# Float32r matmuls read their moving columns from the two halves of a tile in turn

## The chip, the cores and the metric

One core of a Trainium2 chip runs the whole program. The metric is device time in microseconds (us) from launch to the last result, the median of the runs made; lower is better.

## The reference

The inputs are q, k and v of 8 batches, 8 heads, 576 positions and 64 dimensions, and the weights of two feed-forward blocks. A retention layer (attention without softmax, with a decay per head) feeds a maxout block, and that a bilinear block:

```python
def reference(**kwargs):
    # retention: scores = q k^T / sqrt(D), times gamma^(i-j) for j <= i, times v
    x = np.ascontiguousarray(attn_out.transpose(0, 2, 1, 3)).reshape(B * S, H * D)  # 4608 x 512
    # maxout: d_ff = 768
    h = np.maximum(np.maximum(x @ w1, x @ w2), x @ w3)
    x = h @ w_out
    # bilinear: d_ff = 1024
    a = x @ w1
    b = x @ w2
    h = a * b @ w3
    return (h @ w_out).astype(np.float32)
```

## The kernel before

The kernel works in stages, and in all of them TensorE (PE) does the products, ScalarE (ACT) and VectorE (DVE) read the results out of the PSUM banks, and GpSimd (POOL) takes some of the elementwise work.

**How one product is made.** The retention itself (lines 343 to 404) uses plain float32 matmuls. Everything behind it uses the type float32r: each operand is split into a high part (a copy rounded to float32r, `copy_r`, line 92) and a low part (the remainder, `low`, line 95), and a product of two operands is three matmuls, high by high, low by high, high by low, that all add into one PSUM bank. A matmul has a stationary operand (128 columns, loaded first) and a moving operand that streams past it, 512 or 256 columns wide. In memory the moving columns stand next to each other, four bytes each.

**The stages.** (1) For each of 9 blocks of 512 tokens, `products` (line 478) multiplies the token block, the moving operand, with the three maxout weights; 12 matmuls of 512 columns fill a bank, and `maximum` (line 488) reads it: a copy by ACT for the first weight, a maximum by DVE for the other two. In between PE makes the retention products of the next block. An order written out by hand (`ORDER`) sets the first two blocks, and due times the rest. (2) The product with `w_out` of the maxout block, as a fast matrix product with seven multiplications in place of eight (`Z_ORDER`, line 526), in five groups of tokens, four with 512 columns and one with 256. `snap_z` and `keep_z` (lines 765 and 770) read the banks. (3) The product of the two last weights, `ps_w` (line 912), 192 matmuls of 512 columns. (4) The two bilinear factors, again with seven products (line 1176), in ten visits, eight with 512 columns and two with 256; `snap`, `plus` and one multiplication (lines 1154, 1159 and 1209) read the banks. (5) The last product (`add_o`, line 1223), in 18 steps of 84 matmuls of 256 columns; `snap_o`, `plus_o` and a copy (lines 1231, 1236 and 1283) read the banks.

All matmuls of stages 2 to 5 are issued by one helper, `product` (line 709, the matmul on line 715), those of stage 1 on line 486. PE works its matmuls off in the order written. The first stage has six banks for the products, the later ones eight, so that the reading of one bank lies beside the filling of others.

Of the kernel before, what the change touches and what calls it, by code (L numbers as in the profile page):

```python
# [13 lines left out]
AF = mybir.ActivationFunctionType  # L14
ALU = mybir.AluOpType
# [72 lines left out]
def tile_retention_maxout_bilinear(ctx: ExitStack, tc, a, out):  # L88
    nc = tc.nc
    chunks = chunk_list()  # L90

    def copy_r(dst, src):
        nc.scalar.activation(dst, src, AF.Copy)  # L93
# [3 lines left out]

    def load(dst, src):
        nc.sync.dma_start(out=dst, in_=src)  # L99

    first_ps = ctx.enter_context(ExitStack())
    ps_mm = first_ps.enter_context(tc.tile_pool(name="ps_mm", bufs=6, space=PSUM))
# [17 lines left out]
    def bank(name):  # L120
        return ps_mm.tile([P, 512], F32, tag="mm", name=name)
# [75 lines left out]
    w1h = [w1_p.tile([P, 3, 4, P], F32R, name=f"w1h{f}") for f in range(KF1)]  # L197
    w1l = [w1_p.tile([P, 3, 4, P], F32R, name=f"w1l{f}") for f in range(KF1)]
# [279 lines left out]
    def products(t, f, i, cols):  # L478
        xh, xl = xs[t]
        ps = hbs[t, f, i, cols.start] = bank("ps_h")  # L480
        mms = []
        for c in range(4):
            mms += [(w1h[f][:, i, c], xh[:, c, cols]), (w1l[f][:, i, c], xh[:, c, cols])]
        mms += [(w1h[f][:, i, c], xl[:, c, cols]) for c in range(4)]
        for n, (l, r) in enumerate(mms):
            nc.tensor.matmul(ps[:, cols], l, r, start=n == 0, stop=n == len(mms) - 1)  # L486

    def maximum(t, f, i, cols):
        ps = hbs.pop((t, f, i, cols.start))
        if (t, f) not in hbs:  # L490
            hbs[t, f] = hb_p.tile([P, N1], F32, tag="hb", name="hb")
        hb = hbs[t, f][:, cols]
        if i == 0:
            copy_r(hb, ps[:, cols])
        else:
            nc.vector.tensor_tensor(hb, ps[:, cols], hb, ALU.max)  # L496

    def keep(t, f):
        load(h_d[t][:, f], hbs.pop((t, f)))
# [129 lines left out]
    with tc.manual_schedule():  # L629
# [79 lines left out]
        def product(ps, terms, start=True, stop=True, again=False):  # L709

            mms = []
            for lh, ll, rh, rl in terms:
                mms += [(lh, rh), (ll, rh), (lh, rl)]
            for j, (l, r) in enumerate(mms):
                nc.tensor.matmul(ps, l, r, start=start and j == 0, stop=stop and j == len(mms) - 1, skip_group_check=again)  # L715
# [48 lines left out]

        def snap_z(ps, size):
            t = zo_p.tile([P, N1], F32, tag="zs", name="zs", bufs=6)[:, :size]
            nc.scalar.activation(t, ps[:, :size], AF.Copy)
            return t

        def keep_z(j, m, n, ps, other=None):  # L770
            size = z_groups[j][3]
            o = zo_p.tile([P, N1], F32, tag="zo", name="zo", bufs=4)[:, :size]
            if other is None:
                nc.scalar.activation(o, ps[:, :size], AF.Copy)
            else:
                nc.vector.tensor_tensor(o, ps[:, :size], other, ALU.add)
            load(z_d[j][:, m, n * size:n * size + size], o)

        behind_z = {0: [(h_t4, 0)], 1: [(load_h, 1, "b12")], 2: [(load_h, 1, "b21")], 3: [(h_t3, 1), (load_h, 2, "b22")],
# [1 line left out]
        for j, (_, _, _, size) in enumerate(z_groups):  # L781
            Z = {}
            saved = {}
            for n, (x, y) in enumerate(Z_ORDER):
# [4 lines left out]
                ps = Z[bank_of]  # L789
# [115 lines left out]
        ps_w = []  # L905
        for n in range(2 * KF2):
            k, e = divmod(n, 2)
            th, tl = w3t.pop(n)
            for m in range(4 * e, 4 * e + 4):
                if k == 0:  # L910
                    ps_w.append(bank8(f"ps_w{m}"))
                product(ps_w[m], [(th[:, m % 4], tl[:, m % 4], *wo2[k])], k == 0, k == KF2 - 1)
                if k == KF2 - 1:
                    t = w4_p.tile([P, DM], F32, tag="w4", name="w4")
                    copy_r(t, ps_w[m])
                    load(w4_d[:, m], t)
            prepare_34(*[(get_w3t, n + 4)] * (n + 4 < 2 * KF2), *[(get_wo2, k + 2)] * (e == 0 and k + 2 < KF2), lag=2)
            lows()
            if steps:
                steps.pop(0)()  # L920
# [202 lines left out]
        for n, (k, q) in enumerate(visits):  # L1123
            B, size = ops[k % 2], z_groups[k][3]
            if n == 5:
                steps = steps + fetches(visits[7][0])
            elif n == 9:
                steps = steps + late[1]
            elif n != 4:
                steps = steps + rest.pop()  # L1130
                if n == 3:
                    second_q = second_sums()
                    steps += second_q.pop(0)
                elif n == 8:
                    late = last_operands()
                    steps += late[0]
                else:
                    steps += fetches(visits[n + 2][0]) + 3 * [waiting]

            left_ticks = [14]  # L1140

            def tick():
                if n == 4 and left_ticks[0] == 7:
                    steps.extend(second_q[0])
                left_ticks[0] -= 1
                lows()
                for _ in range(1 if n in (4, 5) else 3 if n == 3 or n in (0, 1, 2, 6, 7) and left_ticks[0] % 2 or n == 9 and left_ticks[0] % 2 else 2):
                    if steps:
                        step = steps.pop(0)
                        step()  # L1150
                        if step is waiting:
                            break

            def snap(ps):
                t = work("snap", 5)[:, :size]
                nc.scalar.activation(t, ps[:, :size], AF.Copy)  # L1156
                return t

            def plus(ps, t):
                r = work("c", 6)[:, :size]  # L1160
                nc.vector.tensor_tensor(r, ps[:, :size], t, ALU.add)  # L1161
                return r

            def keep_g(t, half, cols):
                off = half * z_groups[k][2]
                load(g_d[z_groups[k][half]][:, cols, off:off + size], t)

            def times(x, y):
                nc.gpsimd.tensor_tensor(x, x, y, ALU.mult)  # L1169
                return x  # L1170

            for o in (2 * q, 2 * q + 1):
                fs = slice(o % 2 * P, (o % 2 + 1) * P)
                X, V, Y = ([bank8(f"ps_{x}{i}") for i in range(2)] for x in "xvy")

                def add(ps, x, y, start):
                    for i in range(2):
                        (ah, al), (bh, bl) = wsum[i][q][x], B[y]
                        product(ps[i][:, :size], [(ah[:, c, fs], al[:, c, fs], bh[:, c, columns(size)], bl[:, c, columns(size)]) for c in range(2)],
                                start, True, not start)  # L1180

                add(X, "a11", "b11", True)
                p1 = [snap(X[i]) for i in range(2)]
                tick()
                add(V, "a12", "b21", True)
                c11 = [plus(V[i], p1[i]) for i in range(2)]
                tick()
                add(X, "s2", "t2", False)
                g11 = times(*c11)
                u2 = [snap(X[i]) for i in range(2)]  # L1190
                tick()
                add(Y, "s1", "t1", True)
                p5 = [snap(Y[i]) for i in range(2)]
                tick()
                add(X, "s3", "t3", False)
                keep_g(g11, 0, o)
                c22 = [plus(X[i], p5[i]) for i in range(2)]
                g22 = times(*c22)
                tick()
                add(Y, "s4", "b22", False)  # L1200
                c12 = [plus(Y[i], u2[i]) for i in range(2)]
                keep_g(g22, 1, 4 + o)
                g12 = times(*c12)
                tick()
                add(X, "a22", "t4", False)
                c21 = snap(X[0])
                keep_g(g12, 1, o)
                g21 = work("c", 6)[:, :size]
                nc.vector.tensor_tensor(g21, X[1][:, :size], c21, ALU.mult)
                keep_g(g21, 0, 4 + o)  # L1210
                tick()
        for step in steps:
# [17 lines left out]

        def snap_o(ps):
            t = work("snap", 5)[:, :256]
            nc.scalar.activation(t, ps[:, :256], AF.Copy)
            return t

        def plus_o(dst, ps, t):
            nc.vector.tensor_tensor(dst, ps[:, :256], t, ALU.add)

        def open_s(s):

# [13 lines left out]
        for s in range(n_s):  # L1254
            X, V, Y = banks.pop(s)
            ob = obs.pop(s)
# [23 lines left out]
                plus_o(ob[0][:, 256:], Y, u2)  # L1280
                load(out[2 * turn[s] * P:(2 * turn[s] + 1) * P, :], ob[0])
            add_o(X, "a22", "t4", False, s)
            nc.scalar.activation(ob[1][:, :256], X[:, :256], AF.Copy)
            cols = slice(0, DM if s + 1 < n_s else 256)
            load(out[(2 * turn[s] + 1) * P:(2 * turn[s] + 2) * P, cols], ob[1][:, cols])
            gq.pop(s)
# [28 lines left out]
```

## Time and profile before

| | us |
|---|---|
| median of 3 runs | 1266.95 |
| lowest and highest of them | 1266.43, 1274.92 |
| span of the profiled execution | 1265.7 |
| PE busy in it | 1256.2 |
| DVE busy | 885.5 |
| ACT busy | 488.1 |
| POOL busy | 314.1 |

The profile is of one execution, traced from the first to the last instruction; that distance is its span. A matmul's duration in the trace, from its start to its modelled end, is longer than the distance between the starts of two matmuls, since they overlap; the pace is read from the starts, or from a stretch that holds many of them. Idle time of an engine is listed with what ended it.

### The profile page before, as it was taken

The page shows a single profiled execution, that of the slowest core. Times are in us where ns is not written, and L with a number is a line of the kernel's source. Part 1 is how long each engine was busy: PE and PEld are TensorE (multiplying, and loading weights), DVE is VectorE, ACT ScalarE, POOL GpSimd, SP SyncE. Part 2 cuts the span into 40 slices and gives each one's busy share as a digit, 9 for nine tenths or more (in the row PEclk, how much of TensorE's full clock was granted, in tenths as well). Part 3 has the DMA queues.
Part 4 walks back from the last instruction along what each step waited for, and adds up shares of the span by engine and source line. Part 5 has one row for each costly group of instructions (what it writes and reads, how often), then busy time and mean ns, then how long its engine had stood idle before and what let it go on. Part 6 is the DMA issues. An engine that isn't in the chain of part 4 may idle for free.

```text
span 1265.7 us, 22992 instructions
## 1 busy us (share of the span) xinstructions
PE 1256.2 (99%) x8900; PEld 1079.0 (85%) x8900; DVE 885.5 (70%) x1256; ACT 488.1 (39%) x873; POOL 314.1 (25%) x262
## 2 busy tenths in 40 slices
PE   8999999999999999999999999999999999999999
PEld 6888888888888878888888888888998888999998
DVE  5885667666666666366988547776666766899896
ACT  4551122222222212134565454443344343555554
POOL 2111211212111210000000315544243542344443
PEclk9999999999999999999999999999999999999999
DMA  9945788777978795434743733332333314455552
GB/s 210 244 119 118 148 210 211 178 207 182 246 180 175 166 198 154 166 109 151 225 174 122 236 110 125 116 124 103 110 113 133 117 51 160 131 176 159 167 175 101
DMA packets 323793, 199.34 MB, mean 157 GB/s; under 512 B 241634, under 2 KB 279266, under 8 KB 323684
## 3 DMA queue, kind: packets, MB, share of 16 engines
q1 hardware_dynamic: 323684, 197.87, 56.2%
q8 instruction: 70, 1.15, 0.4%
q14 instruction: 39, 0.32, 0.1%
HBM read 131.76 MB, written 66.06 MB: 156 GB/s over the span
## 4 chain that ended last, share of the span: by engine, by line
PE 91%; DMA 3%; DVE 2%; SPq 2%; issue 1%; ACT 1%; POOL 0%; DVEq 0%; POOLq 0%; ACTq 0%
PE ps_h L486 32%; PE ps_x L715 23%; PE ps_y L715 11%; PE ps_v L715 6%; PE ps_X L715 5%; PE ps_Y L715 3%; PE o L384 2%; PE sc L369 2%; PE ps_w L715 2%; SPq L99 2%; PE ps_V L715 1%; DMA raw<-in_moe_w_dram 1%; PE st L404 1%; PE o L391 1%; DMA w<-wo_d 1%
## 5 line engine op out<-in xcount | busy, mean ns | idle before, releaser
L486 PE MATMUL ps_h<-xh,w1h 128*128 128x512 f32 (+1 forms) x664 | 257.3, 389 | 0.0
L486 PE MATMUL ps_h<-xh,w1l 128*128 128x512 f32 (+1 forms) x664 | 254.4, 385 | 0.6 <-DVE w1l L96 0.6
L486 PE MATMUL ps_h<-xl,w1h 128*128 128x512 f32 (+1 forms) x664 | 174.1, 384 | 0.0
L486 PEld LDWEIGHTS ps_h<-xh,w1h 128*128 128x128 f32 x664 | 124.6, 188 | 27.6 <-issue 2.1
L486 PEld LDWEIGHTS ps_h<-xh,w1l 128*128 128x128 f32 x664 | 124.7, 188 | 25.0 <-DVE w1l L96 0.9
L486 PEld LDWEIGHTS ps_h<-xl,w1h 128*128 128x128 f32 x664 | 123.0, 188 | 24.8
L496 DVE TENSOR_TENSOR hb<-ps_h,hb 128x512 f32<-128x512 f32 (+1 forms) x110 | 74.4, 677 | 93.0 <-PE ps_h L486 85.9
L1169 POOL TENSOR_TENSOR c<-c 128x512 f32<-128x512 f32 (+1 forms) x60 | 84.2, 1405 | 174.4 <-DVE c L1161 132.2
L1156 ACT ACTIVATE snap<-ps_x 128x512 f32<-128x512 f32 (+1 forms) x100 | 55.7, 557 | 174.4 <-PE ps_x L715 174.3
L355 POOL TENSOR_TENSOR q<-q,tables 128x512 f32<-128x512 f32 (+1 forms) x31 | 31.4, 1011 | 282.1 <-DMA q<-in_q_dram 164.3
L166 ACT ACTIVATE e<-raw 128x512 f32<-128x512 f32 x64 | 42.9, 670 | 131.8 <-DMA raw<-in_moe_w_dram 90.7
L93 ACT ACTIVATE hb<-ps_h 128x512 f32<-128x512 f32 (+1 forms) x56 | 32.5, 581 | 134.9 <-PE ps_h L486 134.8
L93 ACT ACTIVATE xh<-o 128x512 fp32r<-128x512 f32 (+1 forms) x40 | 22.2, 555 | 110.1 <-PE o L391 68.5
L358 POOL TENSOR_TENSOR v<-v,tables 128x512 f32<-128x512 f32 x40 | 44.6, 1116 | 63.8 <-DMA v<-in_v_dram 59.2
L1161 DVE TENSOR_TENSOR c<-ps_x,snap 128x512 f32<-128x512 f32 (+1 forms) x40 | 25.3, 638 | 45.7 <-PE ps_x L715 23.3
L376 DVE TENSOR_TENSOR p<-sc,mask 128x512 f32<-128x512 f32 (+1 forms) x80 | 48.0, 627 | 11.9 <-PE sc L369 11.7
L96 POOL TENSOR_TENSOR ol<-raw,oh 128x512 fp32r<-128x512 f32 x1 | 1.3, 1292 | 219.5 <-ACT oh L93 219.5
L172 DVE CUSTOM_DVE_ANT_0 m<-m,r 128x1024 uint16<-128x1024 uint16 x64 | 49.2, 769 | 6.9
L1161 DVE TENSOR_TENSOR c<-ps_v,snap 128x512 f32<-128x512 f32 (+1 forms) x40 | 25.0, 635 | 32.7 <-PE ps_v L715 19.8
L715 PE MATMUL ps_x<-t4h,a 128*128 128x512 f32 (+1 forms) x160 | 45.4, 368 | 0.3 <-DVE a L96 0.3
L715 PE MATMUL ps_x<-b11h,a 128*128 128x512 f32 (+1 forms) x160 | 45.2, 367 | 0.0
L715 PE MATMUL ps_x<-t2h,s 128*128 128x512 f32 (+1 forms) x160 | 45.2, 367 | 0.0
(302 smaller groups left out, 3266.5 us busy)
## 6 DMA issues: line engine op xcount, KB each, us to landing
zr<-g_d SPq DMA_DIRECT2D x18, 1024.0 KB, 6.1
raw<-in_moe_w_dram SPq DMA_DIRECT2D x34, 512.0 KB, 5.8
g_d<-c SPq DMA_DIRECT2D x64, 256.0 KB, 2.2
zr<-z_d SPq DMA_DIRECT2D x28, 512.0 KB, 6.2
h_d<-hb SPq DMA_DIRECT2D x54, 256.0 KB, 3.5
b<-h_d SPq DMA_DIRECT2D x16, 768.0 KB, 6.2
out_dram<-ob SPq DMA_DIRECT2D x35, 256.0 KB, 2.1
v<-in_v_dram SPq DMA_DIRECT2D x32, 256.0 KB, 4.2
```

What stands on the lines that cost most here:

```text
L93: nc.scalar.activation(dst, src, AF.Copy)
L166: nc.scalar.activation(z["e"], raw[:, :, 1].bitcast(F32), AF.Copy, scale=2.0 ** -112)
L172: nc.vector.tensor_tensor(z["m"], z["m"], z["r"], ALU.add)
L355: nc.gpsimd.tensor_tensor(z["q"][:, :r], z["q"][:, :r], qs[:, j, :r].unsqueeze(3).to_broadcast([P, r, G, 32]), ALU.mult)
L358: nc.gpsimd.tensor_tensor(z["v"], z["v"], vd.unsqueeze(2).to_broadcast([P, H, D]), ALU.mult)
L376: nc.vector.tensor_tensor(z[g][:c, :, :c], z["sc"][g][:c, :, :c], mask[:c, :c].unsqueeze(1).to_broadcast([c, G, c]), ALU.mult)
L486: nc.tensor.matmul(ps[:, cols], l, r, start=n == 0, stop=n == len(mms) - 1)
L496: nc.vector.tensor_tensor(hb, ps[:, cols], hb, ALU.max)
L715: nc.tensor.matmul(ps, l, r, start=start and j == 0, stop=stop and j == len(mms) - 1, skip_group_check=again)
L1156: nc.scalar.activation(t, ps[:, :size], AF.Copy)
L1161: nc.vector.tensor_tensor(r, ps[:, :size], t, ALU.add)
L1169: nc.gpsimd.tensor_tensor(x, x, y, ALU.mult)
```

## The change

Two views are added. `woven` lets a matmul take its moving columns as column 0 of the tile, column 0 of its second half, column 1, column 1 of the second half, and so on. With 512 columns the two halves begin 1024 bytes apart, with 256 columns 512 bytes. The bank is written in the order in which the columns come, so it holds the two halves interleaved, and `unwoven` lets the instruction that empties the bank read it with a step of two words (8 bytes), first the even words, then the odd ones, which puts the columns back into order. Every float32r matmul gets the first, every reader of such a bank the second. Number, size and order of all instructions, tiles and transfers stay as they are; the plain float32 matmuls of the retention are not touched.

```diff
+    def woven(x):
+        return x.rearrange("p (e n) -> p n e", e=2)
+
+    def unwoven(ps):
+        return ps.rearrange("p (n e) -> p e n", e=2)
+
...
         for c in range(4):
-            mms += [(w1h[f][:, i, c], xh[:, c, cols]), (w1l[f][:, i, c], xh[:, c, cols])]
-        mms += [(w1h[f][:, i, c], xl[:, c, cols]) for c in range(4)]
+            mms += [(w1h[f][:, i, c], woven(xh[:, c, cols])), (w1l[f][:, i, c], woven(xh[:, c, cols]))]
+        mms += [(w1h[f][:, i, c], woven(xl[:, c, cols])) for c in range(4)]
...
         if i == 0:
-            copy_r(hb, ps[:, cols])
+            copy_r(hb, unwoven(ps[:, cols]))
         else:
-            nc.vector.tensor_tensor(hb, ps[:, cols], hb, ALU.max)
+            nc.vector.tensor_tensor(hb, unwoven(ps[:, cols]), hb, ALU.max)
...
             for lh, ll, rh, rl in terms:
+                rh, rl = woven(rh), woven(rl)
                 mms += [(lh, rh), (ll, rh), (lh, rl)]
...
-            nc.scalar.activation(t, ps[:, :size], AF.Copy)
+            nc.scalar.activation(t, unwoven(ps[:, :size]), AF.Copy)
...
-                nc.scalar.activation(o, ps[:, :size], AF.Copy)
+                nc.scalar.activation(o, unwoven(ps[:, :size]), AF.Copy)
             else:
-                nc.vector.tensor_tensor(o, ps[:, :size], other, ALU.add)
+                nc.vector.tensor_tensor(o, unwoven(ps[:, :size]), other, ALU.add)
...
-                    copy_r(t, ps_w[m])
+                    copy_r(t, unwoven(ps_w[m]))
...
-                nc.scalar.activation(t, ps[:, :size], AF.Copy)
+                nc.scalar.activation(t, unwoven(ps[:, :size]), AF.Copy)
...
-                nc.vector.tensor_tensor(r, ps[:, :size], t, ALU.add)
+                nc.vector.tensor_tensor(r, unwoven(ps[:, :size]), t, ALU.add)
...
-                nc.vector.tensor_tensor(g21, X[1][:, :size], c21, ALU.mult)
+                nc.vector.tensor_tensor(g21, unwoven(X[1][:, :size]), c21, ALU.mult)
...
-            nc.scalar.activation(t, ps[:, :256], AF.Copy)
+            nc.scalar.activation(t, unwoven(ps[:, :256]), AF.Copy)
...
-            nc.vector.tensor_tensor(dst, ps[:, :256], t, ALU.add)
+            nc.vector.tensor_tensor(dst, unwoven(ps[:, :256]), t, ALU.add)
...
-            nc.scalar.activation(ob[1][:, :256], X[:, :256], AF.Copy)
+            nc.scalar.activation(ob[1][:, :256], unwoven(X[:, :256]), AF.Copy)
```

## Rows read from the trace of the kernel before

**Rows 1.** The page, part 1: busy us (share), instructions, of two engines.
```profile
PE 1256.2 (99%) x8900; PEld 1079.0 (85%) x8900; DVE 885.5 (70%) x1256; ACT 488.1 (39%) x873; POOL 314.1 (25%) x262
```

**Rows 2.** The page, part 2: granted PE clock in tenths, 40 slices.
```profile
PEclk9999999999999999999999999999999999999999
```

**Rows 3.** Waits of PE, longest and last: total us, times, longest us.
```profile
PE o L391 <- DVE s L412: 1.7, 2, 1.5
...
PE ps_x L715 <- DVE a L96: 0.3, 1, 0.3
```

**Rows 4.** The page, part 4: the chain that ended last, by line.
```profile
PE ps_h L486 32%; PE ps_x L715 23%; PE ps_y L715 11%; PE ps_v L715 6%; PE ps_X L715 5%; PE ps_Y L715 3%; PE o L384 2%; PE sc L369 2%; PE ps_w L715 2%; SPq L99 2%; PE ps_V L715 1%; DMA raw<-in_moe_w_dram 1%; PE st L404 1%; PE o L391 1%; DMA w<-wo_d 1%
```

**Rows 5.** Pieces of that chain: start us, us, what, matmuls in it.
```profile
509.14 62.79 PE ps_h L486 x276
...
576.05 4.08 PE ps_V L715 x18
...
906.63 2.83 PE ps_x L715 x24
...
1200.04 1.36 PE ps_x L715 x12
```

**Rows 6.** Groups of PE by form: shapes, count, busy us, mean ns.
```profile
L486 PE MATMUL ps_h<-xh,w1h 128*128 128x512 f32 x632 | 248.7, 394 | 0.0
...
L715 PE MATMUL ps_x<-b11h,a 128*128 128x512 f32 x128 | 39.4, 389 | 0.0
...
L715 PE MATMUL ps_w<-oh,th 128*128 128x512 f32 x64 | 24.9, 390 | 0.0
...
L715 PE MATMUL ps_x<-b11l,a 128*128 128x512 f32 x64 | 24.9, 389 | 0.0
...
L715 PE MATMUL ps_x<-kt,a22h 128*128 128x256 f32 x72 | 15.3, 278 | 0.0
...
L715 PE MATMUL ps_x<-wb,a11l 128*128 128x256 f32 x36 | 10.0, 277 | 0.0
...
L715 PE MATMUL ps_X<-hh,za11h 128*128 128x512 f32 x24 | 9.3, 389 | 0.0
...
L486 PE MATMUL ps_h<-xh,w1h 128*128 128x256 f32 x32 | 8.6, 300 | 0.0
...
L715 PE MATMUL ps_x<-t3h,s 128*128 128x256 f32 x32 | 5.8, 280 | 0.0
...
L715 PE MATMUL ps_X<-hh,za11h 128*128 128x256 f32 x6 | 1.7, 281 | 0.0
```

**Rows 7.** Groups of DVE by form: count, busy us, mean ns, idle before.
```profile
L175 DVE SCALAR_TENSOR_TENSOR m<-raw,m 128x512 int32<-128x512 int32 x64 | 44.3, 695 | 0.2
...
L362 DVE STREAM_TRANSPOSE qt<-q 128x512 f32<-128x512 f32 x25 | 27.1, 1086 | 2.3 <-POOL q L355 2.3
...
L96 DVE TENSOR_TENSOR s4l<-zr,s4h 128x512 fp32r<-128x512 f32 x18 | 12.2, 680 | 0.1
...
L229 DVE STREAM_TRANSPOSE w3t<-m 128x512 f32<-128x512 f32 x16 | 11.3, 707 | 20.1 <-DMA w3t_d<-w3t 20.0
```

**Rows 8.** Groups of ACT by form, columns as above.
```profile
L1156 ACT ACTIVATE snap<-ps_x 128x512 f32<-128x512 f32 x80 | 48.0, 599 | 152.9 <-PE ps_x L715 152.7
L166 ACT ACTIVATE e<-raw 128x512 f32<-128x512 f32 x64 | 42.9, 670 | 131.8 <-DMA raw<-in_moe_w_dram 90.7 <-DMA raw<-in_moe_w_out_dram 28.2 <-DVE m L171 6.2
...
L93 ACT ACTIVATE w1h<-m 128x512 fp32r<-128x512 f32 x18 | 11.0, 626 | 12.3 <-DVE m L175 12.3
```

**Rows 9.** Busy us by engine in two stretches, PE clock, DMA share, GB/s.
```profile
600.00:700.00 100.00, 100.00 (x500) 85.19 (x499) 88.45 (x90) 56.80 (x72) 0.00 (x0) 1.00 0.50 168
...
1080.00:1180.00 100.00, 100.00 (x831) 98.15 (x830) 90.02 (x121) 53.39 (x113) 43.05 (x29) 1.00 0.51 161
```

**Rows 10.** Groups of DVE by form, 1080 to 1180 us.
```profile
L1237 DVE TENSOR_TENSOR ob<-ps_v,snap 128x256 f32<-128x256 f32 x10 | 4.1, 414 | 0.1
```

**Rows 11.** Groups of DVE by form, 600 to 700 us.
```profile
L776 DVE TENSOR_TENSOR zo<-ps_Y,zs 128x512 f32<-128x512 f32 x8 | 5.1, 685 | 0.0
...
L776 DVE TENSOR_TENSOR zo<-ps_X,zs 128x512 f32<-128x512 f32 x6 | 3.8, 683 | 0.0
```

## The prediction

> **What bounds the kernel now.** I read the page first, then the waits of PE, then the chain, then PE's groups by form. PE is busy 99% of the span and every other engine far less [rows 1], at a granted clock of 1.00, the 2.4 GHz level, in all 40 slices [rows 2]. A busy PE could still be waiting, so the waits come next: all that PE waited for on other engines is seven entries, of which the first and the last stand here, 6.3 us together, and no entry is a bank that a reader had not yet emptied [rows 3]. The chain that ended last is PE nearly throughout, and its float32r matmuls (lines 486 and 715) alone are 83% of the span, some 1050 us [rows 4]. So time is the number of moving columns times what PE takes for one, plus a remainder.
>
> The pace of one column comes from pieces of that chain [rows 5]. 18 matmuls of 512 columns take 4.08 us, 226.7 ns each; 12 of 256 columns take 1.36 us, 113.3 ns each. Both are 0.4427 ns per column, where the granted 2.4 GHz would be 0.4167 ns. The excess is 13.4 ns on 512 columns and 6.6 ns on 256: it grows with the columns, so it isn't a price per instruction (loading a stationary operand is the same for both widths). It lies in the streaming itself. And it depends on something other than the count: 24 matmuls of 256 columns whose operand begins at another offset take 2.83 us, 117.9 ns each, in the same stream and at the same clock. I read this as reading the moving operand already being what sets the pace, with nothing in hand. That is the observation on which the forecast turns.
>
> How many columns: by form [rows 6], where each row stands for its family (the high part moves twice per product, the low part once). Of 512 columns: three families of 632 on line 486 (1896), seven of 128 and seven of 64 in the bilinear factors (1344), three of 64 for the two last weights (192), 21 of 24 in the maxout output (504): 3936. Of 256: three of 32 on line 486 (96), seven of 32 and seven of half that in the factors (336), 14 of 72 and 14 of 36 in the last product (1512), 21 of 6 in the maxout output (126): 2070. That is 3936 x 512 + 2070 x 256 = 2,545,152 columns, by 0.4427 ns 1126.8 us, 89% of the span. The remainder, 1265.7 - 1126.8 = 138.9 us, is the retention's plain float32 matmuls, PE's idle time and the two ends; the change does not touch it.
>
> **The change part by part.** Nothing is removed, moved or added as an instruction, a wait or a transfer; two access patterns change.
>
> *The readers.* Those of a bank now step 8 bytes in place of 4. The nearest rows are reads with the same step of 8 bytes, from SBUF: DVE's line 175 takes 695 ns for 512 elements against 680 for a contiguous operation [rows 7], ACT's line 166 takes 670 against 626 [rows 8]. No row shows such a step on PSUM. Below, a gain is excluded: the elements stay as many. Above, I take a doubling. By the rows it is 15 to 45 ns per reader; I take these. It costs the sum nothing, as PE waits for no bank [rows 3]: the reading of a bank lies beside the filling of others, and that cover grows if matmuls get longer. Without the cover it is a rival, below. At the very end one ACT copy of 256 elements is open to view, 20 ns by these rows.
>
> *The moving operand.* Two columns that follow each other were 4 bytes apart and are now 1024 or 512 bytes apart. Any 16 bytes that gave four columns in a row give one, then the other half has its turn. No row of before shows PE reading with a step, so I bound it.
> - Below: no price, if what was fetched for each half is kept while the other has its turn: 0.4427 ns. A gain is all but excluded: 0.4167 ns per column is what the clock allows, and nothing in the change brings the pace nearer.
> - Above: each column pays what four adjoining ones paid, 4 x 0.4427 = 1.771 ns, if 16 bytes are fetched anew for every column.
> - Between, from DVE [rows 7]: line 362 transposes 128x512 and writes with a step of 16 bytes, 1086 ns, where line 229 makes the same transpose and writes contiguously, 707 ns. That is 1.54 times, or 379 ns / 512 = 0.74 ns more per element. So a step of 8 bytes is nearly free and one of 16 is not. As a ratio on PE it gives 138.9 + 1.54 x 1126.8 = 1874 us; as an addition, 1.183 ns per column, 138.9 + 3011 = 3150 us. DVE handles about one element per ns where PE handles more than two, so the ratio is too kind to PE, and the addition supposes that PE overlaps no more than DVE.
> [...]
>
> Sum: 2,545,152 x 0.885 ns = 2253.6 us, plus 138.9 = 2392.5 us of span. The median stands 1.25 us above the profiled span (1266.95 against 1265.7), so 2394 us. Matmuls of 512 columns would then start every 453 ns, of 256 every 227 ns. DVE, with 885 us of work, falls to a share of 37%.
>
> [...]
>
> **The rivals.** *Four times:* 16 bytes are fetched for every column, one after the other. For it: PE's pace looks limited by reading already, and two places a power of two apart may get in each other's way. Against it: it allows no overlap at all between the two runs. 138.9 + 4 x 1126.8 = 4646 us of span, 4647 us.
>
> *Not slower:* PE keeps both runs' 16 bytes at hand, so it fetches as many as before. For it: the pattern touches no more memory than before, and in the same order within each half. Against it: no row shows such keeping, and the pace is sensitive to where an operand lies [rows 5]. It decides as soon as two places can be held; the time is 1267 us.
>
> [...]
>
> *The readers become the bound:* this needs the matmuls unchanged. DVE is at 88.5 us of 100 and 90.0 of 100 in its fullest stretches [rows 9]. In the second, three families of about ten readers of 0.41 us [rows 10], doubled, add 12 us and give 102; in the first, some 20 of 0.68 us [rows 11] add 14 and give 102. So it decides only from about 0.35 us (second) or 0.6 us (first) more per reader, and then costs about 2% of some 300 us, 6 us: 1273 us, still within 1%.
>
> *A lower clock:* if PE stalls on reads, the granted clock could fall to its 1.2 GHz level. Where reading sets the pace that changes nothing for these matmuls and up to doubles the retention's part of 138.9 us. It widens the range; for it speaks nothing in [rows 2].
>
> **How the numbers follow.** About twice (2250 to 2500 us: the clock's own 0.833 ns per column gives 2260; 4% for unlucky places, as in 117.9 against 113.3 ns, gives 2483): 0.42. A price around DVE's ratio, 1300 to 2250 us: 0.08. Around DVE's addition, 2500 to 4000 us: 0.09. Four times, 4000 to 4700 us: 0.25. Not slower, with or without slower readers: 0.14. Faster, for a reason that I don't see: 0.02. About 1% is what a measurement of this kernel can tell from no change. So faster 0.02, same 0.14, slower 0.84. The range leaves out the 0.16 of the last two and reaches from the case of DVE's ratio to four times: 1850 to 4700 us. The forecast is 2394 us, its own range 2250 to 2500 us.
>
> **What would show it.** Right: in the chain, 18 matmuls of 512 columns take 8 us where they took 4.08; PE still busy nearly all the time; retention matmuls and weight loads at their old durations; the readers' rows up by less than 50 ns; DVE's waits for PE longer. If 18 matmuls take about 16 us, it is four times; if 4.08, the halves are kept at hand. If the time grows with the matmuls' pace unchanged, PE waits for banks, and the readers' rows show by how much. A clock row below 9 speaks for the last rival. Wrong would be, above all, the step from DVE's accesses to PE's: the trace of before has no stepped read by PE.

## Result and profile after

The kernel became faster, where a loss of almost double the time was forecast: 1229.28 us median against 1266.95 us before, a ratio of 0.9685 (95% interval 0.9649 to 0.9722), 37.7 us less. The prediction was wrong in sign, and the time lies outside its range. The profiled execution (span 1233.5 us) is the slowest of the five timed ones, so the spans show 5.5 us less gain (32.2 us) than the medians.

PE's pace comes first. These are pieces of the chain that ended last, start us, us, what, matmuls in it; [rows 5] are those of before.

```profile
504.27 59.77 PE ps_h L492 x276
...
596.28 3.88 PE ps_V L722 x18
...
1218.40 2.68 PE ps_x L722 x24
```

18 matmuls of 512 columns take 3.88 us, 215.6 ns each, where they took 226.7; those of 256 columns take 111.7 ns (2.68 us / 24) where they took 113.3. The granted clock of 1.00 is worth 0.4167 ns per column: in the first bench below (1.00 from 422.06 to 436.51 us), halves in turn with one stationary column took 7.77 us / 36 for 512 columns and 3.93 us / 36 for 256, so each of the 256 columns more took 0.4167 ns, 2.4 columns per ns. The excess over that (213.3 and 106.7 ns per matmul) fell from 13.4 to 2.3 ns and from 6.6 to 5.0 ns. So most of the excess of before was a price of the contiguous order for 512 columns, and taking the halves in turn avoids it. For 256 columns it avoids only a quarter.

The page's parts 1 and 4: busy us and shares, then the chain by engine and by line. They answer to [rows 1, 4]; the last line is the chain by engine before.

```profile
PE 1214.9 (98%) x8900; PEld 1081.7 (88%) x8900; DVE 909.3 (74%) x1256; ACT 501.4 (41%) x873; POOL 315.2 (26%) x262
...
PE 76%; DMA 9%; SPq 6%; DVE 5%; issue 2%; ACT 1%; POOL 1%; DVEq 0%; POOLq 0%; ACTq 0%
PE ps_h L492 23%; PE ps_x L722 22%; PE ps_y L722 11%; SPq L99 6%; PE ps_v L722 5%; PE ps_X L722 5%; DMA raw<-in_moe_w_dram 2%; PE ps_Y L722 2%; PE ps_w L722 2%; DMA q<-in_q_dram 2%; PE sc L375 1%; PE o L390 1%; DMA raw<-w3t_d 1%; PE ps_V L722 1%; PE o L397 1%
...
PE 91%; DMA 3%; DVE 2%; SPq 2%; issue 1%; ACT 1%; POOL 0%; DVEq 0%; POOLq 0%; ACTq 0%
```

PE's busy time fell by 41.3 us and its idle time grew from 9.5 to 18.6 us (span less busy). DVE has 24 us more work although no instruction was added. The chain of this execution runs through transfers and SP's queue as well. Groups of DVE and then of ACT by form show where the added work is (count, busy us, mean ns; compare [rows 7, 8]; the last line of DVE is the reader of line 502 before, there line 496):

```profile
L502 DVE TENSOR_TENSOR hb<-ps_h,hb 128x512 f32<-128x512 f32 x106 | 72.6, 686 | 54.3 <-PE ps_h L492 50.5 <-ACT hh L93 2.9 <-ACT r L173 0.2
L181 DVE SCALAR_TENSOR_TENSOR m<-raw,m 128x512 int32<-128x512 int32 x64 | 50.9, 799 | 0.2
...
L368 DVE STREAM_TRANSPOSE qt<-q 128x512 f32<-128x512 f32 x25 | 37.8, 1512 | 8.1 <-POOL q L361 8.1
...
L496 DVE TENSOR_TENSOR hb<-ps_h,hb 128x512 f32<-128x512 f32 x106 | 72.8, 686 | 92.5 <-PE ps_h L486 85.9 <-ACT hh L93 3.1 <-ACT e L166 1.2
```

```profile
L172 ACT ACTIVATE e<-raw 128x512 f32<-128x512 f32 x64 | 52.4, 818 | 187.5 <-DMA raw<-in_moe_w_dram 99.8 <-DMA raw<-in_moe_w_out_dram 53.5 <-DVE qt L368 12.6
...
L1163 ACT ACTIVATE snap<-ps_x 128x512 f32<-128x512 f32 x80 | 47.8, 597 | 139.2 <-PE ps_x L722 130.5 <-DVE t1l L96 3.8 <-DVE wb L96 3.4
```

The readers of the banks, which now step 8 bytes in PSUM, take what they took (DVE 686 ns in both, ACT 597 against 599). What became slower was not edited at all: operations of DVE and ACT that step through SBUF. The transposes went from 1086 to 1512 ns, ACT's reads with a step of 8 bytes from 670 to 818, DVE's from 695 to 799.

Where PE's idle time grew is seen in two stretches of stage 1 (length, PE busy, then the other engines, granted clock, DMA share, GB/s). Before, PE was busy for 25.00 and 24.77 us of the same stretches, at a clock of 1.00.

```profile
200.00:225.00 25.00, 22.54 (x232) 19.21 (x231) 16.20 (x25) 8.17 (x13) 4.95 (x4) 0.93 0.78 207
...
425.00:450.00 25.00, 21.73 (x169) 18.19 (x166) 16.85 (x28) 6.06 (x10) 4.66 (x6) 0.86 0.95 188
```

What PE waited for there is DVE. Of its waits in the whole span by engine and line (total us, times, longest us) the first is the state, 1.7 us before [rows 3]; 2.5 us of it lie in the first stretch, 0.6 in the second.

```profile
PE o L397 <- DVE s L418: 5.7, 6, 2.5
```

### The profile page after: what moved, and what is told of

It is laid out like the page before. It is cut to its first block, busy times and chain, and to the rows that moved or that the text cites. A ratio compares the mean times of both kernels' runs of the same rounds, so it can differ in the third digit from the quotient of the medians.

```text
span 1233.5 us, 22974 instructions
## 1 busy us (share of the span) xinstructions
PE 1214.9 (98%) x8900; PEld 1081.7 (88%) x8900; DVE 909.3 (74%) x1256; ACT 501.4 (41%) x873; POOL 315.2 (26%) x262
## 4 chain that ended last, share of the span: by engine, by line
PE 76%; DMA 9%; SPq 6%; DVE 5%; issue 2%; ACT 1%; POOL 1%; DVEq 0%; POOLq 0%; ACTq 0%
PE ps_h L492 23%; PE ps_x L722 22%; PE ps_y L722 11%; SPq L99 6%; PE ps_v L722 5%; PE ps_X L722 5%; DMA raw<-in_moe_w_dram 2%; PE ps_Y L722 2%; PE ps_w L722 2%; DMA q<-in_q_dram 2%; PE sc L375 1%; PE o L390 1%; DMA raw<-w3t_d 1%; PE ps_V L722 1%; PE o L397 1%
## 5 line engine op out<-in xcount | busy, mean ns | idle before, releaser
L492 PE MATMUL ps_h<-xh,w1h 128*128 128x512 f32 (+1 forms) x664 | 251.9, 381 | 0.3 <-ACT w1h L93 0.3
L492 PE MATMUL ps_h<-xh,w1l 128*128 128x512 f32 (+1 forms) x664 | 249.2, 377 | 0.3 <-DVE w1l L96 0.3
L492 PE MATMUL ps_h<-xl,w1h 128*128 128x512 f32 (+1 forms) x664 | 168.3, 376 | 0.0
L172 ACT ACTIVATE e<-raw 128x512 f32<-128x512 f32 x64 | 52.4, 818 | 187.5 <-DMA raw<-in_moe_w_dram 99.8
L173 ACT ACTIVATE r<-raw 128x512 int32<-128x512 uint32 x64 | 50.8, 794 | 0.6 <-DVE m L178 0.6
L181 DVE SCALAR_TENSOR_TENSOR m<-raw,m 128x512 int32<-128x512 int32 x64 | 50.9, 799 | 0.2
L177 DVE TENSOR_SCALAR m<-e 128x512 int32<-128x512 int32 x64 | 30.1, 470 | 28.3 <-ACT e L172 28.2
L368 DVE STREAM_TRANSPOSE qt<-q 128x512 f32<-128x512 f32 (+1 forms) x31 | 40.7, 1314 | 9.0 <-POOL q L361 9.0
```

The lines of the kernel that those rows point to most:

```text
L172: nc.scalar.activation(z["e"], raw[:, :, 1].bitcast(F32), AF.Copy, scale=2.0 ** -112)
L173: nc.scalar.activation(z["r"], raw[:, :, 0].bitcast(U32), AF.Copy, scale=2.0 ** -29)
L181: nc.vector.scalar_tensor_tensor(z["m"], z["hi"], -0x80000000, z["m"], ALU.bitwise_and, ALU.bitwise_or)
```

## Experiments

Before means a median of 1266 to 1271 us in all of them; a ratio to the kernel before, with its 95% interval, goes with each version that was timed several times. The theories at the start: (A) a contiguous stream gets in its own way, (B) loading the stationary operand takes the cycles, (C) the other engines' reads take them.

**One part alone.** The edit in stages 2 to 5 only (line 486 and its readers as before), and in stage 1 only:

```diff
--- early_only (and the readers of stages 2 to 5 without unwoven)
             for lh, ll, rh, rl in terms:
-                rh, rl = woven(rh), woven(rl)
--- late_only (and maximum without unwoven)
-            mms += [(w1h[f][:, i, c], woven(xh[:, c, cols])), (w1l[f][:, i, c], woven(xh[:, c, cols]))]
-        mms += [(w1h[f][:, i, c], woven(xl[:, c, cols])) for c in range(4)]
+            mms += [(w1h[f][:, i, c], xh[:, c, cols]), (w1l[f][:, i, c], xh[:, c, cols])]
+        mms += [(w1h[f][:, i, c], xl[:, c, cols]) for c in range(4)]
```

> The full kernel with halves in turn in stages 2 to 5 alone (product); stage 1 as before. If the gain is the pace of the matmuls alone: 2040 x 10.9 ns + 1974 x 1.6 ns = 25 us less than before, some 1242 us, as few of ACT's and DVE's stepped operations lie in these stages. If the woven reads cost other engines something there too, less than 20 us is gained.

> The full kernel with halves in turn in stage 1 alone (line 486); the others as before. By the pace alone 1896 x 10.9 ns = 21 us less, 1246 us. If the slower stepped operations of DVE (transposes 1071 to 1516 ns) hold up the retention and through it PE, 8 to 13 us of that are given back: 1253 to 1260 us, with PE waiting for DVE at the state output and the scores. If stage 1 gave nothing at all, 1267 us.

Stages 2 to 5: 1241.3 us, ratio 0.9805 (0.9788 to 0.9821), 25 us, as the pace alone gives. Stage 1: 1250.2 us, ratio 0.9872 (0.9856 to 0.9889), 16 us of the 21 that the pace would give. So it is stage 1 that gives part back, 5 us, where I expected 8 to 13. In its profile PE waited 1.6 us for the state, as before, so that wait alone does not explain the part given back.

**A bench of orders.** Streams of 36 matmuls on one core, first alone, then beside ACT and DVE:

```python
"halves":   x.rearrange("p (e n) -> p n e", e=2)            # A0 B0 A1 B1 ...
"pairs":    x.rearrange("p (e n j) -> p n e j", e=2, j=2)   # A0 A1 B0 B1 ...
"step2":    x.rearrange("p (n e) -> p e n", e=2)            # 0 2 4 ... 1 3 5 ...
"near4":    x.rearrange("p (g e n) -> p g n e", e=2, n=4)   # 0 4 1 5 2 6 3 7, 8 12 ...
```

> None of the reference is computed: the kernel is a bench of 25 streams of 36 matmuls each, one stream per way of reading the moving operand, first with the other engines at rest, then with ACT and DVE streaming copies and transposes, contiguous and stepped in turn. Read from it: the pace of one matmul (first to last start over 35) of each stream, and the mean of the four ACT and DVE operations beside each stream. In the full kernels contiguous columns gave 226.7 ns and halves in turn 215.8 ns per 512. Theory A, the contiguous stream gets in its own way (adjoining columns come from one place, and one cycle in 16 is lost there): contiguous stays at 226 to 227 ns with the other engines at rest, and with one stationary column too; pairs or quads in turn lie between 216 and 227. Theory B, reading the stationary operand takes the cycles: with one stationary column contiguous falls to 216. Theory C, the other engines' reads take them: contiguous is at 216 while they rest and at 227 beside them. On the other engines: if each column of the woven stream is a fetch of its own, ACT's and DVE's stepped operations are slower beside halves than beside contiguous (as 670 to 818 and 1071 to 1516 ns in the full kernels), and pairs and quads take back part of that; if it comes from elsewhere, they are alike.

PE's timeline (start us, length, stream, count; the pace is the distance between two starts over the matmuls between them). The first two lines are of the first part, the others of the second; c512w and halvesw have one stationary column (c512w then 32), c256w and halves256w too:

```profile
168.19 16.84 PE L99 MATMUL a_c512w<-xr,wr 128*1 128x512 f32 x72
184.87 7.93 PE L99 MATMUL a_halvesw<-xr,wr 128*1 128x512 f32 x36
...
253.32 7.93 PE L142 MATMUL b_halves<-xr,wr 128*128 128x512 f32 x36
261.09 10.36 PE L142 MATMUL b_quarters<-xr,wr 128*128 128x512 f32 x36
271.29 12.41 PE L142 MATMUL b_pairs<-xr,wr 128*128 128x512 f32 x36
283.52 9.18 PE L142 MATMUL b_quads<-xr,wr 128*128 128x512 f32 x36
292.54 8.81 PE L142 MATMUL b_blocks<-xr,wr 128*128 128x512 f32 x36
301.18 48.57 PE L142 MATMUL b_step<-xr,wr 128*128 128x512 f32 x108
349.57 15.72 PE L142 MATMUL b_near<-xr,wr 128*128 128x512 f32 x72
...
397.61 16.84 PE L142 MATMUL b_c512w<-xr,wr 128*1 128x512 f32 x72
414.29 7.93 PE L142 MATMUL b_halvesw<-xr,wr 128*1 128x512 f32 x36
422.06 4.48 PE L142 MATMUL b_c<-xr,wr 128*128 128x256 f32 x36
426.38 4.18 PE L142 MATMUL b_halves<-xr,wr 128*128 128x256 f32 x36
430.39 6.29 PE L142 MATMUL b_pairs<-xr,wr 128*128 128x256 f32 x36
436.51 4.37 PE L142 MATMUL b_c256w<-xr,wr 128*1 128x256 f32 x36
440.72 4.09 PE L142 MATMUL b_halves256w<-xr,wr 128*1 128x256 f32 x36
444.65 7.94 PE L142 MATMUL b_bf<-xb,wb 128*128 128x512 bf16 x35
```

Halves: 7.77 us / 36 = 216 ns. Two neighbouring blocks of 4 or 16 columns in turn (near): also 216. Quads in turn 251, blocks of 16 in turn 240, four quarters in turn 283, pairs in turn 340. A step of 2, 4 or 16 columns: 48.39 / 108 = 448 ns in the mean, 451, 460 and 433 one by one. Contiguous with one (and then 32) stationary columns in place of 128: 232 ns, no less than with 128, so (B) falls for 512 columns. For 256 it has a share: one stationary column takes halves from 111 to 109 ns and contiguous from 120 to 117, so a part of the 5.0 ns that stay with halves goes with the size of the stationary operand. The paces of the first part, with ACT and DVE at rest, are the same, so (C) falls. That pairs and quads would lie between 216 and 227, as I expected under (A), was wrong. Two contiguous streams that begin 4 and 32 bytes further on took 235 ns; why contiguous streams take 232 to 235 ns here and 226.7 in the kernel stays open. The plain contiguous one is not usable here, as it ran partly at a granted clock of 0.50 (244.6 to 246.6 us), after PE had waited 2.6 us; the second bench has it.

**A second bench**, for how the order acts and what it does to others:

> A bench, nothing of the reference: 26 streams of 60 matmuls, one per order of the moving columns, all beside ACT and DVE streams as in the first bench. Theory of two paths (the columns at even places and those at odd places of the stream are read by two paths, each keeping one 16-byte piece; two paths in one piece or two places of one bank get in each other's way): eight runs in turn about 448 ns per 512; halves of a twice as sparse tile (step 8 bytes in each run) 240 to 260 ns, and of a four times as sparse one 220 ns or more per 256; each column taken twice, as contiguous or worse. Rival, one path that keeps the last two pieces: the same for eight runs, but each column taken twice as fast as halves, 216. On others' operations: if it is a hop by a multiple of 1024 bytes that slows them, hops of 1040 to 1280 leave them near 1070 (DVE) and 665 ns (ACT), and 1024, 1536 and 2048 tell which multiple counts. Contiguous with one stationary operand kept, or with the moving tile changed at each matmul: 226 against 235 ns would show what makes the bench's contiguous pace worse than the kernel's. In bfloat16: contiguous 216, halves 478 as in the first bench, pairs 216 if two columns of two bytes are one fetch.

Two runs in turn stand 1024 bytes apart in hopA, as in the kernel; eighths are eight runs in turn, twice takes each column twice, halvesbytwo and halvesbyfour take every second and every fourth column of each half, bf is bfloat16.

```profile
28.14 13.76 PE L112 MATMUL contiguous<-xr,wr 128*128 128x512 f32 x60
...
68.94 13.11 PE L112 MATMUL hopA<-xr,wr 128*128 128x512 f32 x60
...
250.24 29.48 PE L112 MATMUL eighths<-xr,wr 128*128 128x512 f32 x60
279.52 13.15 PE L112 MATMUL twice<-xr,wr 128*128 128x512 f32 x60
292.51 13.79 PE L112 MATMUL halvesbytwo<-xr,wr 128*128 128x512 f32 x60
306.13 13.97 PE L112 MATMUL halvesbyfour<-xr,wr 128*128 128x256 f32 x60
319.93 13.14 PE L112 MATMUL bfcontiguous<-xb,wb 128*128 128x512 bf16 x60
332.91 29.23 PE L112 MATMUL bfhalves<-xb,wb 128*128 128x512 bf16 x60
361.98 16.43 PE L112 MATMUL bfpairs<-xb,wb 128*128 128x512 bf16 x60
```

By starts over 60: contiguous 226.7 ns, as in the kernel, whether the stationary operand is kept or the tile changed each time. Two runs in turn 215.8, at each of the 14 distances from 16 to 2048 bytes. Eight runs in turn 488. Each column twice 216.5. The halves of a tile with a step of 8 bytes in each half 227.0, with a step of 16 bytes 230 per 256 columns, thus 460 per 512. In bfloat16 it is the other way round: contiguous 216, pairs in turn 271, halves in turn 484.

My figure for eight runs was right in size, that for the step of 16 bytes too; for the step of 8 bytes I expected 240 to 260, and each column twice I expected to be as slow as contiguous or slower. What fits most of the float32r streams is a count: take the columns at even places of the stream and those at odd places as two streams of their own, and count how many columns in a row each takes from the same 16 bytes. Four (halves, near, twice): 216 ns. Two (contiguous, halves by two): 227. One (step of 2 to 16 columns, halves by four, eighths): 433 to 488. The 16 bytes are the size that these runs pick: with 8, contiguous and a step of 2 would count alike (227 and 451 ns), with 32, contiguous and blocks of 4 (227 and 216). A count over the whole stream doesn't fit: a step of 2 takes two columns of each 16 bytes in a row and still 451 ns. That float32r columns are read by two paths is inferred from this; no row shows the paths. The rival, one path that keeps two pieces, is not excluded by the stream that takes each column twice, but gives contiguous and halves the same number of fetches, and they differ (226.7 and 215.8 ns). Quads and blocks of 16 (two in a row, yet 251 and 240), pairs and quarters (one in a row, yet 340 and 283) and bfloat16 show that the count is not all.

The other engines beside these streams, first for contiguous columns (28.14 to 41.74 us), then for the halves 1024 bytes apart (68.94 to 81.89 us), then for neighbouring blocks of 64 bytes (198.44 to 211.39 us), groups by form:

```profile
L103 DVE STREAM_TRANSPOSE dve_step<-dr 128x512 f32<-128x512 f32 x9 | 9.5, 1053 | 0.0
L100 ACT ACTIVATE act_step<-dr 128x512 f32<-128x512 f32 x13 | 8.5, 652 | 0.0
...
L105 DVE STREAM_TRANSPOSE dve_cont<-dr 128x512 f32<-128x512 f32 x10 | 6.6, 665 | 0.0
```

```profile
L103 DVE STREAM_TRANSPOSE dve_step<-dr 128x512 f32<-128x512 f32 x7 | 10.5, 1495 | 0.0
L100 ACT ACTIVATE act_step<-dr 128x512 f32<-128x512 f32 x11 | 9.3, 849 | 0.0
L101 ACT ACTIVATE act_cont<-dr 128x512 f32<-128x512 f32 x10 | 6.1, 614 | 0.0
L105 DVE STREAM_TRANSPOSE dve_cont<-dr 128x512 f32<-128x512 f32 x7 | 5.2, 737 | 0.0
```

```profile
L103 DVE STREAM_TRANSPOSE dve_step<-dr 128x512 f32<-128x512 f32 x9 | 9.7, 1078 | 0.0
L100 ACT ACTIVATE act_step<-dr 128x512 f32<-128x512 f32 x13 | 8.9, 683 | 0.0
```

Runs 256, 512, 1024, 1280, 1536 or 2048 bytes apart slow the stepped operations to 1465 to 1532 ns (DVE) and 849 to 870 (ACT); runs 16 to 128 bytes apart leave them at 1062 to 1115 and 676 to 683, near the 1053 and 652 beside contiguous columns. 1040 to 1152 bytes lie between, 1139 to 1247 and 668 to 671. ACT's contiguous copy takes 614 to 644 throughout, but DVE's contiguous transpose goes from 665 to 737 to 754 at the multiples of 256, and to 679 to 833 at 1040 to 1152. So the stepped operations suffer most at these multiples of 256 bytes, DVE at 1040 to 1152 too, and 16 to 128 bytes leave both nearly alone.

**Another order in the full kernel**, even columns first, then odd ones:

```diff
     def woven(x):
-        return x.rearrange("p (e n) -> p n e", e=2)
+        return x.rearrange("p (n e) -> p e n", e=2)
     def unwoven(ps):
-        return ps.rearrange("p (n e) -> p e n", e=2)
+        return ps.rearrange("p (e n) -> p n e", e=2)
```

> The full kernel with another order: first all even columns, then all odd ones, a step of 8 bytes; the readers put them back. In the bench a step gave 448 ns per 512 columns. If columns one after another from new places are what costs, as the prediction had it for every stepped order: 139 + 3936 x 0.448 + 2070 x 0.224 = 2366 us, the loss that was forecast for halves. If any order but contiguous is free in this kernel, 1221 to 1267 us.

```profile
881.33 125.33 PE ps_h L492 x276
...
2303.74 2.75 PE ps_v L722 x12
```

2385.5 us in one run. 454 ns (125.33 us / 276) per 512 columns, 229 per 256: 0.89 ns per column. This is the price that was forecast for halves, and nearly its sum. The granted clock was 1.00 throughout.

**Neighbouring blocks in the full kernel**, which keep the pace and spare the others. The edit is near16's; near4 has n=4:

```diff
     def woven(x):
-        return x.rearrange("p (e n) -> p n e", e=2)
+        return x.rearrange("p (g e n) -> p g n e", e=2, n=16)
     def unwoven(ps):
-        return ps.rearrange("p (n e) -> p e n", e=2)
+        return ps.rearrange("p (g n e) -> p g e n", e=2, n=16)
```

> The full kernel with the same edit in all stages, but the two runs that take turns are neighbouring blocks of 16 columns (64 bytes apart) in place of the halves. In the bench this order had the same pace as halves, 216 ns per 512, and left ACT's and DVE's stepped operations as they were beside contiguous columns. If the 9 us that the halves failed to give come from those slower operations: transposes back from 1516 to some 1070 ns, ACT's stepped reads from 818 to 670, no new waits of PE for DVE in stage 1, and the whole 46 us gained, some 1221 us. If the loss comes from stage 1 running faster against its loads alone, the same 1229 us as with halves.

> As near16, with blocks of 4 columns (16 bytes apart). In the bench 216 ns per 512 and no slower operations of others. As near16, some 1221 us, if the pace is all that counts; if neighbouring 16 bytes got in each other's way in the full kernel, slower than near16.

The transposes in near16:

```profile
L368 DVE STREAM_TRANSPOSE qt<-q 128x512 f32<-128x512 f32 x25 | 27.6, 1104 | 5.3 <-POOL q L361 5.3
```

near16: 1231.1 us, 0.9686 (0.9656 to 0.9717). near4: 1227.2 us, 0.9674 (0.9637 to 0.9712). The transposes are back at 1104 ns (near4: 1089), and nothing is gained over the halves (0.9685) that can be told apart. My theory that the slower operations took back the gain fell.

**Loads and stores of stage 1.** In the full kernels so far (even columns first aside) DVE waits 16 to 26 us for the store of the transposed weights, which have one buffer, and holds up what is queued behind it. A second buffer, under three orders; then, on top, earlier loads of q and k, or the later weights' raw loads on ACT's queue:

```diff
--- near4_two_w3t, halves_two_w3t, before_two_w3t
-            wt = cv.tile([P, 512], F32, tag="w3t", name="w3t", bufs=1)
+            wt = cv.tile([P, 512], F32, tag="w3t", name="w3t", bufs=2)
--- near4_two_w3t_early_qk, on top
-        when(t - 8 + lag, fetch_qk)
+        when(t - 9.5 + lag, fetch_qk)
--- near4_two_w3t_act_queue, on top of near4_two_w3t
-                load(dst, src)
+                if name is None:
+                    nc.scalar.dma_start(out=dst, in_=src)
+                else:
+                    load(dst, src)
```

> Blocks of 4 columns in turn, and two buffers in place of one for the transposed weights of stage 1 (line 234). With one buffer DVE waits for the store of the last one, 24 us in all in near4, 20 us before, and holds up what is queued behind it: transposes, the readers of banks, the state. Theory: stage 1 gave less than the matmuls' pace because the loads and stores and DVE's waits for them set its end once PE is faster; this wait is one of them. Then 3 to 6 us less than near4, 1221 to 1224 us, and PE's waits for DVE fewer. Rival, the wait for the store only moves to the next thing that the SP queue is late with: 1227 us as near4.

> The halves in turn with the same second buffer. If the slower stepped operations of ACT and DVE cost time of their own: 3 us or more above near4_two_w3t. If both orders are held up by the same store alone: equal to it, 1221 to 1224 us.

> The kernel before with the second buffer alone. PE waited 6 us in all there, so at most 2 us less, 1265 to 1267 us. If the buffer gains as much here as with the faster matmuls, the wait isn't what took back the gain.

> As near4_two_w3t, with the loads of q and k due 1.5 products (about 4 us) earlier. POOL waits for q 200 us and more in all and DVE's transposes come right behind it. If their lateness still costs PE something: 1 to 3 us less than near4_two_w3t. If the SP queue is what is late, the earlier loads push others back and nothing is gained.

> As near4_two_w3t, with the raw loads of the later weights in stage 1 (the fetch of convert, line 158) issued on ACT's queue in place of SP's. SP's queue is in the chain that ended last with 6% of the span for halves in turn, 2% before. If it is SP's queue that makes the retention's loads late: 3 to 6 us less, about 1221 us. If the transfers themselves are late, on engines that are 0.8 to 0.9 busy there, the same 1227 us; if ACT's queue now waits for buffers ahead of ACT's own work, more.

near4 with two buffers 1226.6 us (0.9669, 0.9635 to 0.9702), halves 1227.5 (0.9671, 0.9637 to 0.9704), contiguous 1264.8 (0.9979, 0.9958 to 0.9999). The buffer gains 0.6 to 2.7 us, mostly within the intervals, and most with contiguous columns, so this wait is not what took the gain back. Earlier loads: 1233.2 us (0.9713, 0.9677 to 0.9750), 6.6 us more than without them, with intervals that overlap. The transposes' wait for q fell from 6.8 to 0.3 us in it, and nothing was gained. ACT's queue: 1249.4 us (0.9853, 0.9823 to 0.9883), much slower; there PE's longest wait is for ACT, whose reading of a bank was late:

```profile
PE sc L378 <- ACT hb L93: 8.0, 1, 8.0
```

I had expected SP's queue to be late; moving loads off it in this way costs more than it gives, so the run doesn't tell whether the queue or the transfers set the rest.

## Why the prediction was wrong

**What bounds the kernel: right.** PE's float32r matmuls set the time, and 2,545,152 columns times their pace plus a remainder is the right sum: even columns first came to 0.89 ns per column and 2385.5 us. That its 454 ns meet the 453 forecast for halves is luck: the forecast priced two runs in turn, and even columns first is one run with a step. The remainder, which "the change does not touch", grew from 138.9 to some 154 us in the profiled execution, by the waits and the clock below.

**The excess of 0.026 ns per column: seen, and read wrongly.** I noted that it grows with the columns, lies in the streaming and depends on where an operand lies, and concluded that reading has nothing in hand. The same row leaves open that the contiguous order itself costs the 6%, which another order might not. The support from the offset doesn't hold either: in the last product the same moving tiles took 117.9 ns (2.83 us / 24) in the second step and 113.3 (2.72 us / 24) in the third (kernel before, as in [rows 5]).

```profile
1107.22 2.83 PE ps_x L715 x24
1117.08 2.72 PE ps_x L715 x24
```

I wrote that a gain "is all but excluded" since "nothing in the change brings the pace nearer" to the clock, and gave it 0.02. That is the step that failed in sign. At 215.8 ns and 111.7 ns the gain was worth 3936 x 10.9 ns + 2070 x 1.6 ns = 46 us.

**The price of the hop: taken for the wrong order.** The sum prices a column at 0.885 ns, twice the 0.4427 of before. No run shows this term for halves in turn: they took 0.421 ns per column (215.8 / 512). It was an estimate that had only its place between the two figures from DVE's stepped writes (0.682 and 1.183 ns per column), in which each element goes to a new place and none returns, and it is the term of the sum that failed. In halves the two places take turns, so each 16 bytes can be used up over the next visits; that they are kept for that is inferred. Doubling is what a step costs (454 ns), two runs in turn cost nothing. The rival "not slower" had the idea that comes nearest (what was fetched for each half is kept), with 0.14; the "four times" rival, with 0.25, had nothing behind it in the runs: the slowest stream, eight runs in turn, took 488 ns, and two places a power of two apart were not in each other's way (215.8 ns at 256, 512, 1024 and 2048 bytes).

**The readers: right in what they cost the sum, too dear in size.** I took 15 to 45 ns for each; the rows show none (DVE 686 before and after). SBUF's step of 8 bytes was not the right neighbour for PSUM.

**What else runs: not considered.** That a reading order on PE could slow stepped operations of ACT and DVE stood nowhere in the prediction. They became up to 40% slower, and it turned out to cost nothing that can be measured.

**The clock: the rival's effect is there, small, by another way.** Slow reads alone did not lower the granted clock: it was 1.00 in even columns first, at half the pace. It fell where PE had waited (0.86 and 0.93 in two stretches, and 0.50 in the first bench after a wait of 2.6 us). In the profiled execution: 46 us by the pace, less 9.1 us of added idle time, less some 5 us by the clock (0.07 and 0.14 of two stretches of 25 us) gives 32 us, and the spans differ by 32.2. The medians differ by 37.7 us.

**Open:** what holds up the retention in stage 1 once the matmuls are faster. It is mostly in stage 1 (16 of 21 us there, 25 of 25 elsewhere; the two parts gain 41 us in sum, both at once 38), it isn't the slower stepped operations (near4 and near16 give no more) and not the one buffer. PE's added waits in the profiled execution are for DVE (the state, 5.7 us against 1.7) and its chain shows transfers and SP's queue (6%), but neither is in every version: stage 1 alone has 1.6 us of the first, halves with two buffers 2% of the second. Earlier loads of q and k gained nothing, and another queue for the raw loads made it worse. No version ran that beats the changed kernel by more than the intervals.

## What to carry to other kernels

Where the pace of a stream per column lies above the granted clock (here 0.4427 against 0.4167 ns) and the excess grows with the columns, ask whether the order itself costs it, before reading it as a limit: an excess is room as well. Price an access order by a row with the same order: steps that never return and runs that take turns are different things (454 and 215.8 ns per 512 columns), and so are two types (two runs in turn took float32r from 226.7 to 215.8 ns, bfloat16 from 216 to 484). When an engine's reading changes, see what the unedited operations of the others take; runs 16 to 128 bytes apart kept the pace and left them nearly as they were, though that gained no time here.

## What was new on the hardware

Contiguous float32r columns took 226.7 ns per 512, two runs in turn 215.8, at all 14 distances tried from 16 to 2048 bytes; a step 433 to 460, eight runs in turn 488. At 256 columns two runs in turn took 111.7 ns against 113.3 in the kernel. In bfloat16 contiguous took 216 and two runs in turn 484. Reading PSUM with a step of 8 bytes cost DVE and ACT nothing (686 ns before and after; 599 and 597). PE reading two runs 256, 512, 1024, 1280, 1536 or 2048 bytes apart slowed DVE's and ACT's stepped operations in SBUF (at 1024 bytes from 1053 to 1495 ns and from 652 to 849) and, less, DVE's contiguous transposes (665 to 737), and left ACT's contiguous copies as they were (620 and 614).
